# Pairs 6 and 7 moved by DMA as well, and another order of steps, in a chunked attention followed by a multiplicative feed-forward layer

## The chip, the core and the metric

The kernel runs on one core of one Trainium2 chip. The metric is the device time of the whole kernel in microseconds: 244.46 us, the median of 3 runs (244.41 to 244.48).

## What is computed

```python
def _attn_ref(q, k, v):                       # 8 batches, 8 heads, 576 rows, 64 wide
    B, H, S, D = q.shape
    chunk = 64
    nc = S // chunk                            # 9 chunks in each batch
    scale = 1.0 / np.sqrt(D)
    ...
    scores = scale * np.matmul(q_c, k_c.transpose(0, 1, 2, 4, 3))
    scores = scores - np.max(scores, axis=-1, keepdims=True)
    attn = np.exp(scores)
    attn = attn / (np.sum(attn, axis=-1, keepdims=True) + 1e-09)
    out = np.matmul(attn, v_c)
    return out.reshape(B, H, S, D)

def _moe_ref(x, w1, w2, w3, w_out):            # 4608 tokens, 512 -> 1024 -> 1024 -> 512
    a = x @ w1
    b = x @ w2
    h = a * b @ w3
    return h @ w_out

x = attn_out.transpose(0, 2, 1, 3).reshape(B * S, H * D)
```

## The kernel before

The 4608 tokens are cut into 18 *pairs* of 256 tokens (four chunks of 64), and two pairs make a *group* of 512. Pairs 0 to 3 go through the feed-forward layer one by one, later ones a group at a time, under the name of the group's first pair (4, 6, 8, to 16). There is no loop in the usual sense: the string ORDER (lines 9 to 40) lists every step of the kernel, and lines 447 and 448 issue them from left to right. Every instruction is kept in that order on its own engine, so ORDER is five queues woven into one. A step is a letter, a pair (or group) number and, after a point, a part:

- On GpSimd's queue (POOL), loads: `q`, `k`, `v` of a pair (lines 149 and 165, issued at line 98); `i`, `h`, `o` the weights; `x` (line 161) a one-element copy that makes the queue wait until a pair's normalised result is there.
- On VectorE (DVE): `T` transposes q (part 0) or k (part 1) of a pair in 32x32 blocks (line 201); `N` takes the reciprocal of the row sums and multiplies (lines 261 and 264), halves 0 and 1; `X` transposes the result to the layer's input (lines 297 and 305); `M` multiplies the copy of a with b (line 366); `V` transposes w3 (line 407).
- On TensorE (PE), all at line 95: `S` the scores, `P` the weighted sum of v, `A` and `B` the products with w1 and w2 for one eighth of the 1024 columns (of a group; one quarter for a single pair), `W` the product of w3 and w_out into one 1024x512 matrix, `O` the output product of a pair.
- On ScalarE (ACT): `E` the exponential (line 234), `C` the copy of A's result to SBUF (line 351), `Y` the copy of O's result (line 396), `Z` the copy of W's.
- On SyncE (SP), DMAs at line 193: `G` and `H`, below, and `Q`, the store of a pair's output.

The block transposes leave 32 rows of a head on one set of 32 partitions and the other 32 on another. For pairs 0 to 7 the score product runs on such 32-row blocks, two of them added up, 64 products for a pair, and `P` on 32-column blocks, 64 products too. From pair 8 on, `G` (line 205) moves q and k of a group between partitions, part 0 and part 1 with four DMAs of 128 KB each, so that `S` has 32 products of 64 rows, and `P` 32 products of 64 columns; `X` then writes to a tile `xm`, and `H` (line 310) moves it to the layer's input with eight DMAs of 64 KB in two parts. The conditions `p < 8` and `p >= 8` (lines 219, 247, 295, 328 and 360) make the choice.

Buffers set most waits between the engines. PSUM is one pool of four tiles, each of two banks (line 88): one tile serves an `S` until its `E` is done, each half of a `P` until its `N`, an `O` until its `Y`, a `W` until its `Z`, and a column part of the layer from its `A` until its `M`. `A` writes the first half of its tile, `B` the second, `C` reads the first half, `M` the copy and the second half. Copies of a have three buffers (line 350), o_sb two, qkT, qkm and xm two each, xt four, q and k five, v six (line 115; pair p uses buffer p modulo 6).

In the order before, each column part is issued as A, B, C, M.

Of the kernel before, what the change touches and what calls it, by code (L numbers as in the profile page):

```python
# [8 lines left out]
ORDER = """  # L9
R0 R1 v0 q1 k1 i0 v1 i1 i2 q2 k2 v2 i3 q3 k3 v3 q4 k4 v4 o h0 h1 D0.0.0.16.64 K0 T0.0 K1 T0.1 q5 k5  # L10
v5 S0 T1.0 E0 P0 D0.1.0.4.512 T1.1 q6 k6 v6 N0.0 S1 D1.0.0.5.512 X0.0 N0.1 X0.1 A0.0 E1 B0.0 C0.0 P1
M0.0 A0.1 N1.0 X1.0 B0.1 C0.1 N1.1 A0.2 X1.1 B0.2 C0.2 M0.1 A1.0 T2.0 B1.0 C1.0 M0.2 A1.1 T2.1 q7 k7
v7 B1.1 C1.1 M1.0 S2 M1.1 A0.3 E2 T3.0 B0.3 C0.3 P2 M0.3 A1.2 N2.0 X2.0 B1.2 C1.2 N2.1 A1.3 X2.1
B1.3 C1.3 M1.2 A2.0 T3.1 q8 k8 v8 B2.0 C2.0 M1.3 S3 T4.0 A2.1 E3 M2.0 B2.1 T4.1 q9 k9 C2.1 P3 v9
M2.1 A2.2 N3.0 B2.2 C2.2 X3.0 A2.3 N3.1 B2.3 X3.1 C2.3 M2.2 S4 M2.3 A3.0 E4 B3.0 C3.0 A3.1 M3.0 B3.1
C3.1 V0 A3.2 M3.1 B3.2 C3.2 V1 A3.3 M3.2 B3.3 C3.3 V2 W0 M3.3 V3 W1 Z0 V4 V5 W2 Z1 V6 V7 T5.0 Z2 W3
T5.1 q10 k10 T6.0 T6.1 P4 v10 q11 k11 Z3 S5 N4.0 O0 E5 X4.0 N4.1 X4.1 T7.0 O1 T7.1 Y0 Q0 T8.0 P5 v11
q12 k12 Y1 S6 T8.1 O2 Q1 E6 N5.0 X5.0 N5.1 X5.1 O3 T9.0 T9.1 Y2 G4.0 P6 v12 q13 k13 A4.0 N6.0 B4.0
G4.1 Y3 X6.0 N6.1 C4.0 A4.1 X6.1 B4.1 C4.1 M4.0 Q2 S7 Q3 M4.1 A4.2 E7 T10.0 B4.2 C4.2 T10.1 P7 v13
q14 k14 A4.3 M4.2 B4.3 N7.0 C4.3 A4.4 X7.0 M4.3 B4.4 C4.4 N7.1 A4.5 M4.4 B4.5 C4.5 X7.1 S8 M4.5 S9  # L20
E8 A4.6 T11.0 B4.6 E9 T11.1 P8 v14 q15 k15 C4.6 A4.7 M4.6 G5.0 B4.7 C4.7 N8.0 A6.0 M4.7 B6.0 N8.1
C6.0 G5.1 A6.1 X8.0 B6.1 M6.0 C6.1 X8.1 P9 v15 A6.2 M6.1 N9.0 B6.2 C6.2 N9.1 A6.3 M6.2 B6.3 C6.3
X9.0 A6.4 M6.3 B6.4 C6.4 X9.1 A6.5 T12.0 H4.0 B6.5 C6.5 M6.4 A6.6 M6.5 B6.6 T12.1 H4.1 C6.6 S10 S11
M6.6 E10 A6.7 T13.0 B6.7 E11 P10 T13.1 C6.7 O4 M6.7 G6.0 N10.0 N10.1 X10.0 G6.1 P11 Y4 X10.1 O5
N11.0 N11.1 x11 q16 k16 v16 Q4 X11.0 X11.1 T14.0 A8.0 H5.0 Y5 B8.0 T14.1 C8.0 A8.1 M8.0 B8.1 H5.1
C8.1 T15.0 A8.2 B8.2 M8.1 C8.2 T15.1 Q5 A8.3 B8.3 C8.3 M8.2 G7.0 S12 M8.3 S13 E12 A8.4 T16.0 B8.4
E13 G7.1 P12 T16.1 C8.4 A8.5 B8.5 M8.4 C8.5 N12.0 A8.6 M8.5 B8.6 C8.6 N12.1 x12 q17 k17 v17 A8.7
M8.6 B8.7 C8.7 X12.0 P13 M8.7 A10.0 X12.1 B10.0 C10.0 N13.0 A10.1 M10.0 B10.1 N13.1 C10.1 A10.2
X13.0 B10.2 M10.1 C10.2 X13.1 S14 S15 M10.2 E14 A10.3 H6.0 T17.0 B10.3 E15 P14 T17.1 C10.3 A10.4
H6.1 M10.3 B10.4 C10.4 N14.0 A10.5 M10.4 B10.5 G8.0 C10.5 N14.1 A10.6 M10.5 B10.6 C10.6 X14.0 P15  # L30
G8.1 X14.1 A10.7 M10.6 B10.7 N15.0 C10.7 O6 N15.1 M10.7 X15.0 X15.1 H7.0 S16 Y6 S17 O7 E16 E17 H7.1
P16 Y7 O8 Q6 N16.0 Q7 N16.1 X16.0 X16.1 P17 Y8 A12.0 N17.0 Q8 B12.0 N17.1 C12.0 A12.1 X17.0 B12.1
M12.0 C12.1 X17.1 A12.2 M12.1 H8.0 B12.2 C12.2 A12.3 M12.2 B12.3 C12.3 H8.1 A12.4 M12.3 B12.4 C12.4
A12.5 M12.4 B12.5 C12.5 A12.6 M12.5 B12.6 C12.6 A12.7 M12.6 B12.7 C12.7 O9 M12.7 O10 Y9 Q9 A14.0 Y10
B14.0 C14.0 Q10 A14.1 M14.0 B14.1 C14.1 A14.2 M14.1 B14.2 C14.2 A14.3 M14.2 B14.3 C14.3 A14.4 M14.3
B14.4 C14.4 A14.5 M14.4 B14.5 C14.5 A14.6 M14.5 B14.6 C14.6 A14.7 M14.6 B14.7 C14.7 O11 M14.7 O12
Y11 Q11 A16.0 Y12 B16.0 C16.0 Q12 A16.1 M16.0 B16.1 C16.1 A16.2 M16.1 B16.2 C16.2 A16.3 M16.2 B16.3
C16.3 A16.4 M16.3 B16.4 C16.4 A16.5 M16.4 B16.5 C16.5 A16.6 M16.5 B16.6 C16.6 A16.7 M16.6 B16.7
C16.7 O13 M16.7 O14 Y13 Q13 O15 Y14 Q14 O16 Y15 Q15 Y16 Q16 O17
"""  # L40
# [4 lines left out]

@with_exitstack
def first_path(
# [305 lines left out]
    def do_M(p, j):  # L353
        g = p // 2
        if g not in ab_t:
            ab_t[g] = msb.tile([P, FO, GT], bf, tag="ab", bufs=3, name="ab")
# [9 lines left out]
        inorder(nc.vector.tensor_mul(o, view(a_t.pop((p, j))[:]), view(ps_t.pop((p, j))[:, 1, :])))  # L366
# [201 lines left out]
```

## Time and profile before

| | us |
|---|---|
| median of 3 runs | 244.46 |
| span of the profiled execution | 242.9 |
| PE, first to last product | 1.44 to 239.66 |
| DVE busy | 154.3 |
| ACT busy | 85.2 |
| POOL busy | 83.7 |

The profile is of one execution. Its span runs from the first to the last instruction; the time of a run lies a little above it, 1.56 us if the median is set beside this span. The slices of the span, 40 equal ones of 6.07 us each, show busy tenths by engine (9 is 90% or more), the granted TensorE clock and the DMA share:

```
PE   1189989999999999999999999999999999999994
DVE  1756799699799588999998899918540332143000
ACT  2412423423333344425336234162332332322322
POOL 7856976656986345764160230000000000000000
PEclk9999999999999999999999999999999999999999
DMA  6999999999999999999999793735502200400244
```

PE is full from the fourth slice on. DVE is nearly full until slice 25 (about 152 us), where the attention ends, and light behind it. The DMA engines are full until slice 22 (about 133 us), most of it q0, the loads of q, k, v and the weights.

### The profile page before, as it was taken

How to read it: one execution, taken by the hardware profiler on the slowest of the kernel's cores; microseconds unless marked ns; L12 is line 12 of the kernel's file. 1: busy time of each engine (PE TensorE's matmuls, PEld its weight loads, DVE VectorE, ACT ScalarE, POOL GpSimd, SP SyncE). 2: the span in 40 equal slices, each digit the busy share in tenths (PEclk: the TensorE clock that was granted, in tenths of full speed). 3: DMA queues.
4: the chain of work that ended last, by engine and by line, in shares of the span. 5: the costliest groups of instructions: out<-in, count | busy, mean ns of one | idle time of the engine just before them, and what ended most of it. 6: DMA issues, size and time to landing. Idle time of an engine off the chain costs nothing.

```text
span 242.9 us, 6385 instructions
## 1 busy us (share of the span) xinstructions
PE 226.7 (93%) x2753; PEld 120.2 (49%) x2753; DVE 154.3 (64%) x235; ACT 85.2 (35%) x116; POOL 83.7 (34%) x114
## 2 busy tenths in 40 slices
PE   1189989999999999999999999999999999999994
PEld 1147868874445444444444444444444444444443
DVE  1756799699799588999998899918540332143000
ACT  2412423423333344425336234162332332322322
POOL 7856976656986345764160230000000000000000
PEclk9999999999999999999999999999999999999999
DMA  6999999999999999999999793735502200400244
GB/s 173 179 185 181 185 169 200 196 193 171 167 173 218 222 228 259 179 224 196 205 236 223 221 139 91 163 88 209 142 0 89 87 0 0 173 3 1 86 173 173
DMA packets 93597, 37.65 MB, mean 155 GB/s; under 512 B 75008, under 2 KB 86528, under 8 KB 93568
## 3 DMA queue, kind: packets, MB, share of 16 engines
q0 software_dynamic: 82592, 18.88, 83.9%
q1 hardware_dynamic: 9936, 17.83, 24.0%
q10 hardware_dynamic: 1040, 0.52, 0.8%
q8 instruction: 21, 0.34, 0.6%
q14 instruction: 8, 0.07, 0.1%
HBM read 38.80 MB, written 9.44 MB: 199 GB/s over the span
## 4 chain that ended last, share of the span: by engine, by line
PE 72%; DMA 16%; DVE 4%; SPq 3%; POOL 2%; issue 1%; ACT 0%; DVEq 0%; POOLq 0%
PE ab_ps L95 39%; PE o_ps L95 23%; PE w_ps L95 6%; DMA w<-in_moe_w_dram 4%; DMA qkm<-qkT 3%; SPq L193 3%; DMA qk<-in_q_dram 3%; DMA qk<-in_k_dram 3%; DMA xt<-xm 3%; PE pv L95 2%; PE s_ps L95 2%; DVE qkT L201 2%; POOL vbuf L98 1%; POOL w L98 1%; DVE xt L297 1%
## 5 line engine op out<-in xcount | busy, mean ns | idle before, releaser
L95 PE MATMUL ab_ps<-xt,w 128*128 128x512 bf16 (+1 forms) x688 | 127.4, 342 | 0.7 <-DVE xt L297 0.6
L95 PEld LDWEIGHTS <-w 128*128 128x128 bf16 x704 | 67.1, 98 | 56.1 <-issue 1.8
L366 DVE TENSOR_TENSOR ab<-a_sb,ab_ps 128x512 bf16<-128x512 f32 x71 | 47.8, 674 | 43.4 <-ACT a_sb L351 43.1
L351 ACT COPY a_sb<-ab_ps 128x512 f32<-128x512 f32 x71 | 41.6, 586 | 81.3 <-PE ab_ps L95 81.0
L95 PE MATMUL o_ps<-w3o,ab 128*128 128x512 bf16 (+1 forms) x296 | 63.9, 373 | 0.0
L201 DVE STREAM_TRANSPOSE qkT<-qk 128x1024 bf16<-128x1024 bf16 x36 | 45.1, 1291 | 7.2 <-ACT qk L144 5.5
L95 PEld LDWEIGHTS <-ab 128*128 128x128 bf16 x296 | 28.5, 98 | 32.2
L98 POOL DMA_DIRECT2D vbuf<-in_v_dram x40 | 33.9, 855 | 20.4 <-DMA qk<-in_q_dram 5.2
L396 ACT COPY o_sb<-o_ps 128x1024 f32<-128x1024 f32 x17 | 17.2, 1012 | 45.3 <-PE o_ps L95 41.3
L264 DVE TENSOR_TENSOR xn<-pv,rcs 128x512 bf16<-128x512 f32 x36 | 24.9, 692 | 1.4
L98 POOL DMA_DIRECT2D qk<-in_q_dram x23 | 18.1, 790 | 8.9 <-DMA qk<-in_k_dram 2.4
L98 POOL DMA_DIRECT2D qk<-in_k_dram x23 | 18.0, 783 | 6.5 <-DMA vbuf<-in_v_dram 3.7
L234 ACT ACTIVATE e<-s_ps 128x1024 bf16<-128x1024 f32 x16 | 15.9, 1026 | 1.7 <-PE s_ps L95 1.3
L95 PE MATMUL w_ps<-wo,w3T 128*128 128x512 bf16 x64 | 14.0, 379 | 0.0
L305 DVE STREAM_TRANSPOSE xm<-xn 128x512 bf16<-128x512 bf16 x20 | 13.5, 696 | 0.2
L261 DVE RECIPROCAL rcs<-pv 128x8 f32<-128x8 f32 x36 | 6.9, 193 | 10.4 <-PE pv L95 10.4
L98 POOL DMA_DIRECT2D w<-in_moe_w_dram x16 | 11.1, 695 | 5.3 <-DMA wo<-in_moe_w_out_dram 2.9
L95 PEld LDWEIGHTS <-e 64*32 64x32 bf16 (+1 forms) x832 | 7.8, 97 | 8.7 <-issue 6.9
L95 PE MATMUL pv<-vbuf,e 64*32 64x65 bf16 (+1 forms) x832 | 10.2, 197 | 1.8 <-ACT e L234 1.1
L297 DVE STREAM_TRANSPOSE xt<-xn 128x512 bf16<-128x512 bf16 x16 | 11.4, 711 | 0.5
L389 DVE COPY o_sb<-o_ps 128x256 f32<-128x256 f32 x1 | 0.4, 425 | 16.0 <-PE o_ps L95 16.0
L95 PEld LDWEIGHTS <-qkT 32*64 32x64 bf16 x512 | 5.5, 117 | 10.1 <-DVE qkT L201 7.9
(29 smaller groups left out, 54.2 us busy)
## 6 DMA issues: line engine op xcount, KB each, us to landing
out_dram<-o_sb SPq DMA_DIRECT2D x17, 512.0 KB, 3.3
qkm<-qkT SPq DMA_DIRECT2D x40, 128.0 KB, 4.0
vbuf<-in_v_dram POOLq DMA_DIRECT2D x32, 128.0 KB, 8.2
w<-in_moe_w_dram POOLq DMA_DIRECT2D x16, 256.0 KB, 9.9
qk<-in_q_dram POOLq DMA_DIRECT2D x11, 256.0 KB, 6.8
qk<-in_k_dram POOLq DMA_DIRECT2D x11, 256.0 KB, 7.8
xt<-xm SPq DMA_DIRECT2D x40, 64.0 KB, 3.2
wo<-in_moe_w_out_dram POOLq DMA_DIRECT2D x4, 256.0 KB, 7.1
```

Source lines behind the costliest of these rows:

```text
L95: return inorder(nc.tensor.matmul(*a, **kw))
L98: return inorder(nc.gpsimd.dma_start(dst, src))
L193: inorder(nc.sync.dma_start(dst, src))
L201: inorder(nc.vector.transpose(qkT_t[g][:, :, p % 2, s, heads(h)].rearrange("p e h (y t) -> p h t e y", t=2), qk_t[p][:, s, heads(h)].rearr ...
L234: inorder(nc.scalar.activation(e_t[p][:, :, heads(hh)], s_t[p][:].rearrange("p u (h q) -> p u h q", q=CH)[:, :, heads(hh)], Exp, scale=sca ...
L261: inorder(nc.vector.reciprocal(rc, pv[:, :, :, D:W]))
L264: inorder(nc.vector.tensor_mul(xn_t[p][:, u], pv[:, :, :, 0:D], rc.to_broadcast([P, 2, 4, D])))
L297: inorder(nc.vector.transpose(new_xt(g)[:].rearrange("p (o t) -> p o t", o=KO)[:, :, t0:t0 + UT] .rearrange("p o (m y) -> p m o y", y=BL), ...
L305: inorder(nc.vector.transpose(xm_t[g][:, u, :, m].rearrange("p o (c y) -> p c o y", y=BL), xn_t[p][:].rearrange("p u r m d -> p (u r) m d" ...
L351: inorder(nc.scalar.copy(a_t[p, j][:], ps_t[p, j][:, 0, :]))
L366: inorder(nc.vector.tensor_mul(o, view(a_t.pop((p, j))[:]), view(ps_t.pop((p, j))[:, 1, :])))
L396: inorder(nc.scalar.copy(o_sb[:], ps_t.pop(p)[:]))
```

## The change

The constant MOVED, 6, takes the place of 8 in the five conditions, so pairs 6 and 7 (group 3) use the moved form: S and P of 32 products, X into xm, and the steps G3.0, G3.1, H3.0, H3.1. The v buffers are handed out from a list in the order in which P gives them back. The string ORDER is written anew: for each letter the pairs come in the same order as before, but the letters are woven together in another way.

```diff
+MOVED = 6
...
+    vb_t, vb_free = {}, list(vbuf)
+
     def load_v(p):
+        vb_t[p] = vb_free.pop(0)
...
-                load(vbuf[p % 6][at * CH:(at + m) * CH, u, :, 0:D],
+                load(vb_t[p][at * CH:(at + m) * CH, u, :, 0:D],
...
-            if p < 8:
+            if p < MOVED:
...
         e = e_t[p]
+        vb_free.append(vb_t[p])
...
-                               rhs=vbuf[p % 6][half[r], u, 2 * g + m % 2, 0:W], start=True, stop=True)
+                               rhs=vb_t[p][half[r], u, 2 * g + m % 2, 0:W], start=True, stop=True)
...
-        if p >= 8:
+        if p >= MOVED:
```

The order is the same up to B0.2. Its lines behind that, as far as they are needed here (two of the old ones, then new ones):

```diff
-M0.0 A0.1 N1.0 X1.0 B0.1 C0.1 N1.1 A0.2 X1.1 B0.2 C0.2 M0.1 A1.0 T2.0 B1.0 C1.0 M0.2 A1.1 T2.1 q7 k7
-v7 B1.1 C1.1 M1.0 S2 M1.1 A0.3 E2 T3.0 B0.3 C0.3 P2 M0.3 A1.2 N2.0 X2.0 B1.2 C1.2 N2.1 A1.3 X2.1
...
+M0.0 A0.1 N1.0 X1.0 B0.1 C0.1 N1.1 A0.2 X1.1 B0.2 M0.1 C0.2 A1.0 A1.1 B1.0 T2.0 T2.1 q7 B1.1 S2 M0.2
+C1.0 C1.1 A0.3 E2 M1.0 P2 k7 B0.3 M1.1 A1.2 N2.0 C0.3 A1.3 B1.2 N2.1 X2.0 T3.0 C1.2 B1.3 X2.1 T3.1
+C1.3 A2.0 M0.3 C2.0 B2.0 M1.2 q8 S3 A2.1 M1.3 A2.2 M2.0 E3 P3 T4.0 C2.1 C2.2 B2.1 N3.0 B2.2 N3.1
...
+T6.0 E4 T6.1 Z2 P4 T7.0 S5 T7.1 N4.0 Z3 k10 O0 T8.0 O1 q11 E5 N4.1 X4.0 Y0 G3.0 q12 X4.1 Y1 k11 P5
+v8 N5.0 N5.1 O2 Q0 X5.0 X5.1 G3.1 A4.0 O3 T8.1 C4.0 Y2 S6 E6 S7 T9.0 T9.1 Q1 B4.0 T10.0 M4.0 A4.1
+G4.0 T10.1 E7 P6 Y3 B4.1 v9 N6.0 C4.1 N6.1 A4.2 G4.1 C4.2 B4.2 M4.1 X6.0 M4.2 A4.3 P7 q13 q14 N7.0
+Q2 B4.3 C4.3 A4.4 N7.1 k12 B4.4 M4.3 A4.5 X6.1 C4.4 C4.5 B4.5 A4.6 k13 k14 C4.6 M4.4 A4.7 S8 T11.0
+v10 B4.6 B4.7 M4.5 q15 X7.0 X7.1 M4.6 C4.7 S9 M4.7 E8 P8 N8.0 O4 E9 N8.1 Q3 P9 Y4 H3.0 O5 T11.1 X8.0
+T12.0 H3.1 v11 T12.1 Y5 N9.0 T13.0 A6.0 G5.0 B6.0 N9.1 X8.1 C6.0 X9.0 A6.1 C6.1 B6.1 T13.1 A6.2 B6.2
+X9.1 M6.0 G5.1 A6.3 C6.2 H4.0 H4.1 q16 M6.1 B6.3 A6.4 M6.2 B6.4 C6.3 S10 M6.3 v12 C6.4 G6.0 E10 A6.5
+T14.0 T14.1 M6.4 C6.5 B6.5 A6.6 M6.5 C6.6 B6.6 A6.7 C6.7 P10 M6.6 S11 N10.0 B6.7 A8.0 B8.0 E11 Q4
...
+P13 C10.0 v14 M10.0 C10.1 B10.1 N13.0 N13.1 A10.2 M10.1 X12.0 A10.3 B10.2 X12.1 C10.2 C10.3 q17
+A10.4 M10.2 B10.3 x12 G7.0 B10.4 X13.0 G7.1 C10.4 A10.5 v15 k17 M10.3 X13.1 M10.4 x11 A10.6 S14 S15
+T16.1 T17.0 T17.1 B10.5 C10.5 B10.6 C10.6 E14 O6 M10.5 Q5 M10.6 E15 P14 N14.0 N14.1 G8.0 Y6 X14.0 O7
+Y7 P15 G8.1 A10.7 H6.0 B10.7 S16 C10.7 N15.0 E16 N15.1 X14.1 X15.0 v16 v17 S17 M10.7 O8 E17 H6.1 Q6
+Y8 P16 A12.0 B12.0 N16.0 A12.1 C12.0 M12.0 P17 B12.1 C12.1 N16.1 A12.2 C12.2 X15.1 B12.2 N17.0 H7.0
+A12.3 C12.3 Q7 N17.1 M12.1 B12.3 A12.4 B12.4 M12.2 C12.4 A12.5 B12.5 M12.3 C12.5 M12.4 A12.6 Q8
...
+C14.7 M14.6 Q11 M14.7 B16.0 A16.1 A16.2 C16.0 A16.3 B16.1 M16.0 C16.1 M16.1 A16.4 C16.2 C16.3 B16.2
+C16.4 M16.2 A16.5 B16.3 O12 Y12 M16.3 C16.5 B16.4 A16.6 O13 Y13 M16.4 A16.7 B16.5 M16.5 C16.6 C16.7
+Q12 B16.6 O14 B16.7 M16.6 Q13 O15 Y14 Q14 Y15 Q15 M16.7 O16 Y16 Q16 O17
```

In the old order the same stretches read `A4.2 E7 T10.0 B4.2 C4.2`, `S8 M4.5 S9 E8 A4.6 T11.0 B4.6 E9 T11.1 P8` and `T17.0 B10.3 E15 P14 T17.1 C10.3 A10.4 H6.1 M10.3`.

More of the change, by code (lines that the diff above doesn't have):

```diff
@@ L16 @@
[L16 to L37, printed above, removed]
@@ L38 @@
-C16.3 A16.4 M16.3 B16.4 C16.4 A16.5 M16.4 B16.5 C16.5 A16.6 M16.5 B16.6 C16.6 A16.7 M16.6 B16.7
-C16.7 O13 M16.7 O14 Y13 Q13 O15 Y14 Q14 O16 Y15 Q15 Y16 Q16 O17
+M0.0 A0.1 N1.0 X1.0 B0.1 C0.1 N1.1 A0.2 X1.1 B0.2 M0.1 C0.2 A1.0 A1.1 B1.0 T2.0 T2.1 q7 B1.1 S2 M0.2
+C1.0 C1.1 A0.3 E2 M1.0 P2 k7 B0.3 M1.1 A1.2 N2.0 C0.3 A1.3 B1.2 N2.1 X2.0 T3.0 C1.2 B1.3 X2.1 T3.1
+C1.3 A2.0 M0.3 C2.0 B2.0 M1.2 q8 S3 A2.1 M1.3 A2.2 M2.0 E3 P3 T4.0 C2.1 C2.2 B2.1 N3.0 B2.2 N3.1
+A2.3 B2.3 X3.0 X3.1 A3.0 M2.1 C2.3 M2.2 k8 A3.1 M2.3 B3.0 B3.1 T4.1 C3.0 q9 M3.0 C3.1 M3.1 A3.2 v7
@@ new lines @@
+T12.0 H3.1 v11 T12.1 Y5 N9.0 T13.0 A6.0 G5.0 B6.0 N9.1 X8.1 C6.0 X9.0 A6.1 C6.1 B6.1 T13.1 A6.2 B6.2
+X9.1 M6.0 G5.1 A6.3 C6.2 H4.0 H4.1 q16 M6.1 B6.3 A6.4 M6.2 B6.4 C6.3 S10 M6.3 v12 C6.4 G6.0 E10 A6.5
+T14.0 T14.1 M6.4 C6.5 B6.5 A6.6 M6.5 C6.6 B6.6 A6.7 C6.7 P10 M6.6 S11 N10.0 B6.7 A8.0 B8.0 E11 Q4
+G6.1 N10.1 C8.0 M6.7 M8.0 X10.0 X10.1 k15 P11 A8.1 A8.2 B8.1 N11.0 B8.2 k16 A8.3 C8.1 C8.2 N11.1
+X11.0 B8.3 A8.4 M8.1 v13 B8.4 S12 C8.3 M8.2 S13 C8.4 H5.0 X11.1 M8.3 A8.5 E12 A8.6 C8.5 M8.4 B8.5
@@ new lines @@
+C8.6 T15.0 H5.1 B8.6 A8.7 B8.7 T15.1 M8.5 E13 P12 M8.6 A10.0 T16.0 B10.0 N12.0 C8.7 A10.1 N12.1 M8.7
+P13 C10.0 v14 M10.0 C10.1 B10.1 N13.0 N13.1 A10.2 M10.1 X12.0 A10.3 B10.2 X12.1 C10.2 C10.3 q17
+A10.4 M10.2 B10.3 x12 G7.0 B10.4 X13.0 G7.1 C10.4 A10.5 v15 k17 M10.3 X13.1 M10.4 x11 A10.6 S14 S15
+T16.1 T17.0 T17.1 B10.5 C10.5 B10.6 C10.6 E14 O6 M10.5 Q5 M10.6 E15 P14 N14.0 N14.1 G8.0 Y6 X14.0 O7
+Y7 P15 G8.1 A10.7 H6.0 B10.7 S16 C10.7 N15.0 E16 N15.1 X14.1 X15.0 v16 v17 S17 M10.7 O8 E17 H6.1 Q6
@@ new lines @@
+Y8 P16 A12.0 B12.0 N16.0 A12.1 C12.0 M12.0 P17 B12.1 C12.1 N16.1 A12.2 C12.2 X15.1 B12.2 N17.0 H7.0
+A12.3 C12.3 Q7 N17.1 M12.1 B12.3 A12.4 B12.4 M12.2 C12.4 A12.5 B12.5 M12.3 C12.5 M12.4 A12.6 Q8
+C12.6 A12.7 H7.1 B12.6 B12.7 O9 C12.7 Y9 M12.5 M12.6 A14.0 B14.0 C14.0 M12.7 M14.0 A14.1 C14.1 A14.2
+B14.1 A14.3 X16.0 C14.2 Q9 B14.2 X16.1 O10 Y10 M14.1 X17.0 H8.0 B14.3 A14.4 Q10 C14.3 X17.1 A14.5
+M14.2 B14.4 C14.4 O11 Y11 A14.6 C14.5 M14.3 M14.4 A14.7 H8.1 A16.0 C14.6 B14.5 B14.6 B14.7 M14.5
+C14.7 M14.6 Q11 M14.7 B16.0 A16.1 A16.2 C16.0 A16.3 B16.1 M16.0 C16.1 M16.1 A16.4 C16.2 C16.3 B16.2
@@ L246, in do_P @@
             for m in range(4):
-                if p < 8:
+                if p < MOVED:
                     for g in range(NB) if hh is None else (2 * hh, 2 * hh + 1):
@@ L255, in do_P @@
                         mm(pv[half[g], r, m * W:(m + 1) * W], lhsT=e[half[r], u, 4 * g + m, :],
-                           rhs=vbuf[p % 6][half[r], u, 4 * g + m, 0:W], start=True, stop=True)
+                           rhs=vb_t[p][half[r], u, 4 * g + m, 0:W], start=True, stop=True)
     def do_N(p, u):
@@ L294, in do_X @@
         g, m = divmod(p, 2)
-        if p < 8:
+        if p < MOVED:
             t0 = m * PT + u * UT
@@ L359, in do_M @@
             view = lambda t: t.rearrange("p (j t) -> p j t", j=2)
-        elif p < 8:
+        elif p < MOVED:
             o = ab_t[g][:, j]
```

3 lines of the change are left out of this document (1 added, 2 removed).

## The prediction

> **What bounds the kernel now.** I read the page's busy rows first, then the chain of waits, then the timelines of PE, ACT, DVE and SP. The busy rows and the chain's shares (page, parts 1 and 4):
>
> ```profile
> PE 226.7 (93%) x2753; PEld 120.2 (49%) x2753; DVE 154.3 (64%) x235; ACT 85.2 (35%) x116; POOL 83.7 (34%) x114
> ...
> PE 72%; DMA 16%; DVE 4%; SPq 3%; POOL 2%; issue 1%; ACT 0%; DVEq 0%; POOLq 0%
> ```
>
> PE is busy for all but 16 us of 242.9. The PE timeline puts 11.3 us of that ahead of 24.3 us and 3.2 us behind the last product (239.66); between, PE stands still for about 1.6 us. So from 24.3 us on, whatever PE does not do is a gain, and whatever holds PE is a loss of the same size. The step prices come from the chain (start, us, what) and the PE timeline:
>
> ```profile
> 187.82 13.81 PE ab_ps L95 x64
> ...
> 74.14 0.72 PE L95 MATMUL pv<-vbuf,e 64*32 64x65 bf16 x64
> 74.79 0.71 PE L95 MATMUL s_ps<-qkT 32*64 32x64 bf16 x64
> ...
> 130.50 0.71 PE L95 MATMUL s_ps<-qkm 64*64 64x64 bf16 x64
> ...
> 132.97 0.45 PE L95 MATMUL pv<-vbuf,e 64*64 64x65 bf16 x32
> ```
>
> One A or B of four 512-column products is 13.81/16 = 0.863 us on PE; one of eight 256-column products (pairs 0 to 3) is 0.89 (64 of them take 7.09 at 45.03). One product lasts 379 ns (the group's mean) and the next starts 216 ns after it, so the last one drains 0.16 us after PE could go on.
>
> What happens behind a product, from one instruction-by-instruction timeline (start, us, engine, line, operation):
>
> ```profile
> 123.50 4.70 PE L95 MATMUL ab_ps<-xt,w 128*128 128x512 bf16 x21
> ...
> 125.42 0.59 ACT L351 COPY a_sb<-ab_ps 128x512 f32<-128x512 f32 x1 [0.71 <-PE ab_ps L95]
> 126.04 0.69 DVE L366 TENSOR_TENSOR ab<-a_sb,ab_ps 128x512 bf16<-128x512 f32 x1 [0.27 <-ACT a_sb L351]
> ```
>
> A8.0 starts at 123.50, so its last product could be followed at 124.36, B8.0's at 125.23. The copy C8.0 reads only A's half of the tile, yet starts at 125.42, after B. So with the order A, B, C the copy waits for B; M ends 1.5 us after B's last issue (0.2 + 0.59 + 0.02 + 0.69). PE meanwhile works on other tiles.
>
> A wait PE to ACT to PE, and a queue held in order:
>
> ```profile
> 10.94 1.03 ACT L234 ACTIVATE e<-z_ps 128x1024 bf16<-128x1024 f32 x1 [2.74 <-PE z_ps L95]
> ...
> 12.02 0.75 PE L95 MATMUL pv<-vbuf,e 64*32 64x65 bf16 x64 [1.13 <-ACT e L234]
> ...
> 30.64 1.31 DVE L201 STREAM_TRANSPOSE qkT<-qk 128x1024 bf16<-128x1024 bf16 x1 [1.32 <-DMA qk<-in_q_dram]
> 31.86 0.65 DVE L366 TENSOR_TENSOR ab<-a_sb,ab_ps 128x512 bf16<-128x512 f32 x1
> ...
> 30.40 0.46 PE L95 MATMUL pv<-vbuf,e 64*32 64x65 bf16 x37
> 31.53 0.30 PE L95 MATMUL pv<-vbuf,e 64*32 64x65 bf16 x27 [0.67 <-issue]
> ```
>
> PE stood 1.13 us for a 1.03 us activation: both hand-overs cost 0.10 together. M0.3 (31.86) stood behind T3.0, which waited for its load, though its copy ended at 31.10: the engines keep their order. The last two rows are P2, held until 31.53 by the last part of v2.
>
> **The change part by part.** All is summed along PE, against the span.
>
> *Less work.* S6 and S7 go from 64 products (0.645 us between neighbours) to 32 (0.32, two pairs are x64 in 0.64); P6 and P7 from 0.63 to 0.38. Together -1.15 us. PE is full there (80 to 90 us), so this is kept.
>
> *C between A and B.* The new order often has A C B. As C waited for B by tile, not by half, so B's first product now waits for C: the built program has this wait at 27 of the B steps and at none before. Price of a bare site (B next after A on PE): drain 0.16 + copy 0.59 + hand-overs 0.10 = 0.85 us. Between 0.59 (copy alone) and 0.95 (with a weight load of 98 ns); I take 0.85, since the wait is on the product, its weights loaded. Bare are B2.0, B4.2, B4.5, B6.1, B6.6, B12.2, B12.3: 7 x 0.85 = +5.95. At B6.5 ACT first does C6.4 (0.59) and E10 (1.03), then C6.5: B6.4's end + 0.2 + 0.59 + 1.03 + 0.6 + 0.05 = 2.5, against S10 and A6.5 (1.2): +1.25. Partly covered: B10.1 (P13's 0.38 of 0.85) +0.4; B10.3 and B16.2, where ACT does C10.2 or C16.1 first, which wait for the B before: 1.46 against one A of 0.86, +0.6 each; B6.7 and B16.6 +0.1 each. Sum +1.8. The other 14 have at least one whole A or other work of 0.86 in between and cost nothing.
>
> Row and rule: the row 125.42 shows a copy that waits for a product in the other half. The Trainium skill (PSUM — Partial Sum Buffer, "PSUM bank collisions raise a hardware error") asks only for guards by bank and quadrant, and the halves are two banks; by it no B need wait, and these 9.0 us would be nothing.
>
> *ACT's order.* C4.7 now stands ahead of E8. C4.7 waits for B4.7, E8 only for the earlier S8. P8 needs E8: 0.2 + 0.59 + 1.03 + 0.05 = 1.87 after B4.7; PE has S9 (0.32): +1.55.
>
> *DVE's order.* T16.1, T17.0, T17.1 now stand between M10.4 and M10.5, and O6 takes the PSUM buffer that M10.5 frees. M10.4 ends 1.5 after B10.4, three transposes at 1.2 (four in 4.80 at 69.53), M10.5 0.6: 5.7. PE has A10.5, A10.6, S14, S15, B10.5, B10.6: 4.1. +1.65. P17 takes the buffer that M12.0 frees, 1.5 after B12.0, with only A12.1 (0.86) between: +0.65. Likewise A8.2 behind M8.0 +0.2, and P6 behind E6 and E7 +0.1.
>
> *P2 ahead of B0.3.* v2's loads and all before are unchanged, so P2's second half still begins at 31.53, but B0.3 (0.89) no longer lies in front: +0.98; the 0.29 us that A2.0 waited for X2.1 goes, T3.0 having moved behind X2.0: net +0.7.
>
> *SP.* G3 and H3 are new: 8 moves each, 128 and 64 KB. At 0.63 to 0.9 us an issue and 3 to 4 us to land they need 9 to 11 us from the last transpose. Along PE's new order G3 (from T7.1, about 69) has 15 us to S6, G4 (82) 16 to S8, H3 (98) 12 to A6.0, H4 16, G5 13. H5 has 7 from X11.1 to A10.0, with 6.5 needed (four issues, the other four gone out after X11.0, and 3.2); H6 stands behind G8, which waits for T17.1, and has about 0.5 to spare at A12.0. Q0 to Q8 are past or between them and hold 0.5 each. I take 0. The bounds are these:
>
> ```profile
> xt<-xm SPq DMA_DIRECT2D x40, 64.0 KB, 3.2
> ...
> 126.97 6.53 DMA xt<-xm
> ```
>
> With 6.53 instead of 3.2, up to +6 at A10.0, S16 and A12.0.
>
> *POOL.* Loads are issued in a new order with the same buffers. q7 to k9 go ahead of v8, so T7.0 may wait about 1 us for q7 on DVE; N4.0 behind it is 1.8 ahead of O1, so PE sees nothing. q13 waits for T8.1 (80), 30 us ahead of T13.0. x12 now gates v15, k17: k17 goes out 3.3 us after N12.1 and lands within 7.8 (median); T17.1 comes 12.5 after. If later, O6 waits as much longer.
>
> *Sum.* -1.15 + 5.95 + 1.25 + 1.8 + 1.55 + 1.65 + 0.95 + 0.7 = +12.7. Span 242.9 + 12.7 = 255.6. The runs' median is 1.56 above the profiled span (244.46), the profiled run's own time is not on the page; I add the same: **257.2 us**.
>
> **Rivals.** (1) *The copies cost nothing* (0.08): B does not stand for C, as two banks would allow. The 9.0 us of the second part go: 248.2. For it: the halves never overlap. Against: 125.42, and the built waits.
>
> (2) *Late moves* (0.11): the 6.53 of a move among loads at A10.0, S16 and A12.0: 263. Against: x12 holds the loads back, so the queue is empty there.
>
> (3) *The queues do not hold* (0.04): ACT and DVE take what is ready, so C4.7 does not hold E8, T17.1 not M10.5, and the copies are through before PE asks. Then only the work counts: -1.15, and the 0.67 and 0.29 of idle: 242.4, faster. It decides if all new stands together are under 2.1 us. Against: M0.3 behind T3.0.
>
> (4) *The clock falls* (0.03): after the 7.36 us that PE stood at the start, nine 512-column products took 489 ns on average instead of 379, 1 us in all. If each of some 13 stands did so: 270. Against: they are under 1.7 us, and the granted clock reads 9 in all 40 slices. The Trainium skill (TensorE: Matmul & The Clock Gate, "A second HAM failure mode: psum-queue depth-cycling") tells of short gaps between groups that make the clock swing; no row here shows it.
>
> **How the numbers follow.** Forecast 0.74 (own range 254 to 260.5: eight sites at 0.59 and O6 1 us less, or half of the late moves). Left out below are rivals 1 and 3 (0.12), above rival 4 and the far half of 2, so 251.5 to 262.5. Same means within 0.2% (0.5 us), about what a measurement can tell: 0.02, between rival 3 and the rest; faster 0.04; slower 0.94.
>
> **What would show it.** In the new profile PE idle before ab_ps products with releaser ACT a_sb L356, 0.7 us each and 0.85 from pitch, at the sites named; one idle of 1.5 before a pv (ACT e) near 101 us and one before o_ps (DVE ab) near 160; a chain with ACT a_sb in it several times, where now it is 0%. PE busy should fall by about 1. It is wrong if PE runs on through B4.2, or if the gaps stand instead behind SP's moves.

## The result, and the profile after

| | before | after |
|---|---|---|
| median of the runs, us | 244.44 (244.24 to 244.48) | 254.46 (254.1 to 255.28) |
| ratio to before, 95% interval | | 1.0416 [1.0396, 1.0437] |
| profiled execution: its own time, us | not shown (median of the first three 244.46) | 255.28 |
| its span, us | 242.9 | 253.7 |
| last product ends, us | 239.66 | 250.44 |

The kernel became 4.2% slower. The median grew by 10.0 us; the span of the profiled execution, the longest of the four, by 10.8, and all of it lies before the end of the last product. The busy rows and the chain's shares of the kernel after (page, parts 1 and 4):

```profile
PE 228.2 (90%) x2625; PEld 119.2 (47%) x2625; DVE 154.0 (61%) x235; ACT 83.7 (33%) x116; POOL 83.7 (33%) x114
...
PE 78%; DVE 8%; ACT 6%; DMA 4%; issue 2%; DVEq 0%; SPq 0%
...
L96 PE MATMUL ab_ps<-xt,w 128*128 128x512 bf16 (+1 forms) x688 | 129.7, 342 | 7.8 <-ACT a_sb L356 6.3
```

No engine got more to do: DVE, ACT and POOL are as busy as before, and PE has 128 products less. PE's busy time did not fall, since the page counts the drain of the last product before each stand as busy (some 0.16 us each time). ACT, which had 0% of the chain, has 6%. The last line is the group of all w1 and w2 products: PE stood 7.8 us ahead of them, 6.3 of it for `a_sb`, the copy of A's result, which no step but M reads.

Where PE stands, from its timeline (start, us, what, products; in brackets the idle time before and what ended it):

```profile
31.36 0.27 PE L96 MATMUL pv<-vbuf,e 64*32 64x65 bf16 x19 [1.09 <-issue]
...
102.23 0.45 PE L96 MATMUL pv<-vbuf,e 64*64 64x65 bf16 x32 [1.23 <-ACT e L238]
...
110.87 2.75 PE L96 MATMUL ab_ps<-xt,w 128*128 128x512 bf16 x12 [0.69 <-DMA qkm<-qkT]
...
122.57 1.89 PE L96 MATMUL ab_ps<-xt,w 128*128 128x512 bf16 x8 [0.73 <-ACT a_sb L356]
...
152.68 3.62 PE L96 MATMUL ab_ps<-xt,w 128*128 128x512 bf16 x16 [0.30 <-ACT a_sb L356]
...
160.09 3.61 PE L96 MATMUL o_ps<-w3o,ab 128*128 128x512 bf16 x16 [1.32 <-DVE ab L371]
```

In order these are P2, P8, A6.0, B6.5, B10.3 and O6. Not in the list are B2.0, B4.2, B4.5, B6.1, B6.6, B12.2 and B12.3 (0.67 each, for `a_sb`), and B10.1 and B16.2, which look like B10.3 (0.30 each); P17's second half has 0.28, A12.0 0.21, and P2 another 0.17 ahead of its first product. One site close up, B4.2, with all engines (start, us, engine, what):

```profile
87.69 0.81 PE L96 MATMUL ab_ps<-xt,w 128*128 128x512 bf16 x3
...
88.54 0.58 ACT L356 COPY a_sb<-ab_ps 128x512 f32<-128x512 f32 x1 [0.28 <-PE ab_ps L96]
...
89.17 1.02 PE L96 MATMUL ab_ps<-xt,w 128*128 128x512 bf16 x4 [0.67 <-ACT a_sb L356]
```

A4.2's last product ends at 88.50, the copy C4.2 runs from 88.54 to 89.12, and B4.2 starts at 89.17. B writes the other half of the tile than the copy reads, and still it waits for the whole copy. The wait is written into the program: the trace has, at the first product of B4.2, a wait for a semaphore of ACT, raised at 89.13 as the copy ended.

The stands of the two timelines account for the loss. Each counts with 0.16 us of drain, as the prediction counted it: the 18 stands behind 25 us in after sum to 11.3 + 18 x 0.16 = 14.2, the three in before (P2 0.67, A2.0 0.29, S7 0.49) to 1.45 + 3 x 0.16 = 1.9. With 1.15 us less work the difference is 14.2 - 1.9 - 1.15 = 11.1, against 10.8 measured.

### The profile page after: what moved, and what is told of

The parts are those of the page before. It is cut to its first block, busy times and chain, and to the rows that moved or that the text cites. A ratio compares the mean times of both kernels' runs of the same rounds, so it can differ in the third digit from the quotient of the medians.

```text
span 253.7 us, 6185 instructions
## 1 busy us (share of the span) xinstructions
PE 228.2 (90%) x2625; PEld 119.2 (47%) x2625; DVE 154.0 (61%) x235; ACT 83.7 (33%) x116; POOL 83.7 (33%) x114
## 4 chain that ended last, share of the span: by engine, by line
PE 78%; DVE 8%; ACT 6%; DMA 4%; issue 2%; DVEq 0%; SPq 0%
PE ab_ps L96 43%; PE o_ps L96 22%; PE w_ps L96 5%; ACT a_sb L356 4%; DVE qkT L205 4%; PE z_ps L96 3%; PE pv L96 3%; DMA raw<-in_q_dram 2%; DMA qkm<-qkT 2%; PE s_ps L96 2%; DVE ab L371 2%; ACT e L238 2%; DVE xn L269 1%; DVE xt L302 1%; ACT qk L145 0%
## 5 line engine op out<-in xcount | busy, mean ns | idle before, releaser
L96 PE MATMUL ab_ps<-xt,w 128*128 128x512 bf16 (+1 forms) x688 | 129.7, 342 | 7.8 <-ACT a_sb L356 6.3
L356 ACT COPY a_sb<-ab_ps 128x512 f32<-128x512 f32 x71 | 41.0, 587 | 88.7 <-PE ab_ps L96 85.3
L96 PE MATMUL o_ps<-w3o,ab 128*128 128x512 bf16 (+1 forms) x296 | 64.7, 374 | 1.3 <-DVE ab L371 1.3
L310 DVE STREAM_TRANSPOSE xm<-xn 128x512 bf16<-128x512 bf16 x24 | 16.0, 691 | 0.1
L99 POOL DMA_DIRECT2D w<-in_moe_w_dram x16 | 11.1, 694 | 5.2 <-DMA vbuf<-in_v_dram 2.0
L96 PEld LDWEIGHTS <-w3T 128*128 128x128 bf16 x64 | 6.3, 98 | 7.3
L412 DVE STREAM_TRANSPOSE w3T<-w 128x1024 bf16<-128x1024 bf16 x8 | 9.5, 1225 | 0.1
```

What stands on the lines that cost most here:

```text
L96: return inorder(nc.tensor.matmul(*a, **kw))
L99: return inorder(nc.gpsimd.dma_start(dst, src))
L310: inorder(nc.vector.transpose(xm_t[g][:, u, :, m].rearrange("p o (c y) -> p c o y", y=BL), xn_t[p][:].rearrange("p u r m d -> p (u r) m d" ...
L356: inorder(nc.scalar.copy(a_t[p, j][:], ps_t[p, j][:, 0, :]))
L412: inorder(nc.vector.transpose(w3T_t[f][:].rearrange("p k (f y) -> p f k y", y=BL), w3[:, NB * f:NB * (f + 1), :].rearrange("p f (k x) -> p ...
```

## The experiments

Each was timed against the kernel before on its own chip, so the ratio is what compares them. The orders are given by the steps that move.

**1. All copies behind their B.** In the new order the 28 C steps that stand between their A and B go right behind B; nothing else changes.

```diff
-N6.1 A4.2 G4.1 C4.2 B4.2 M4.1
+N6.1 A4.2 G4.1 B4.2 C4.2 M4.1
...
-A12.3 C12.3 Q7 N17.1 M12.1 B12.3
+A12.3 Q7 N17.1 M12.1 B12.3 C12.3
```

> The changed kernel (254.46) with each of the 28 copies C that stood between A and B moved to just behind its B; nothing else differs. Theory (a product B stands for the copy of its own tile): the eight stands of 0.67 to 0.73 before ab_ps and the three of 0.30 go, each with 0.16 us of drain, 6.0 + 0.9 + 1.8 = 8.7, less up to 1 us where M now frees its PSUM tile 0.6 us later: 246 to 247. Rival (the stands only uncover another limit, the moves between partitions or DVE): a part of it comes back at A6.0, A10.0 or A12.0, 249 or more. Rival (copies cost nothing, it is the weaving): within 1 us of 254.5.

Measured: 248.25 us, ratio 1.0144 [1.0121, 1.0166]: 6.6 us less than after by the ratios (0.0272 x 244.4), 7.2 by the spans of the profiled executions (246.5). PE's stands behind 25 us are now these, and two short ones, 0.16 ahead of P2 and 0.15 ahead of S11:

```profile
31.37 0.27 PE L96 MATMUL pv<-vbuf,e 64*32 64x65 bf16 x19 [1.08 <-issue]
85.93 0.52 PE L96 MATMUL pv<-vbuf,e 64*64 64x65 bf16 x32 [0.47 <-DVE ab L371]
100.35 0.45 PE L96 MATMUL pv<-vbuf,e 64*64 64x65 bf16 x32 [1.23 <-ACT e L238]
108.62 8.79 PE L96 MATMUL ab_ps<-xt,w 128*128 128x512 bf16 x40 [0.32 <-DMA xt<-xm]
154.99 3.61 PE L96 MATMUL o_ps<-w3o,ab 128*128 128x512 bf16 x16 [1.65 <-DVE ab L371]
172.81 0.32 PE L96 MATMUL pv<-vbuf,e 64*64 64x65 bf16 x16 [0.28 <-DVE ab L371]
```

No stand for `a_sb` is left. The eleven of after came to 6.3 + 11 x 0.16 = 8.1 us, and 7.2 of span came back: C4.0, now behind B4.0, makes M4.0 later and costs P6 0.47, and O6 stands 0.33 longer. The time lies between the 246 to 247 expected and the first rival's 249. About two thirds of the loss is the place of the copies; the rest, some 3.6 us of span, is elsewhere in the new order.

**2 and 3. The same edit in the kernel before.** Only there C goes ahead of B: in group 14 (8 sites), then in groups 12, 14 and 16 (24 sites), where nothing but A, B, C, M and O runs.

```diff
-A14.1 M14.0 B14.1 C14.1 A14.2 M14.1 B14.2 C14.2
+A14.1 M14.0 C14.1 B14.1 A14.2 M14.1 C14.2 B14.2
```

> The kernel before (244.44) with the copies C14.0 to C14.7 put between their A and B: eight bare sites, PE's and DVE's orders untouched. Theory: 8 x 0.84 = +6.7, 251.1, with eight stands of 0.67 us before ab_ps, released by the copy. Rival (the tile's halves are two banks, so B does not stand): 244.4.

> As the last, with the 24 copies of groups 12, 14 and 16: 24 x 0.84 = +20.2, 264.6, three times the effect of eight. Rival (many short stands make the TensorE clock fall): more than that, and a granted clock below 1; rival (no wait): 244.4.

Measured: 251.22 us, ratio 1.0268 [1.0244, 1.0292] with 8 sites, and 265.32, 1.0831 [1.0809, 1.0853] with 24. From the ratios that is 0.0268 x 244.96 / 8 = 0.82 us a site, and 0.0831 x 244.96 / 24 = 0.85: the prediction's price for a bare site, and it adds up site by site. The waits of the 24-site kernel (who waited for what: us in all, times, longest):

```profile
PE ab_ps L95 <- ACT a_sb L351: 17.1, 24, 1.5
```

One stand for each edited site, in a kernel that had none. The granted clock stayed at 1.0 with a stand every 2.56 us. The Trainium skill (PSUM — Partial Sum Buffer, "PSUM bank collisions raise a hardware error") asks for guards by bank and quadrant only; here the two halves of a tile are two banks, and the built program guards them as one. The measurement decides: a copy between A and B costs 0.83 us of PE's time, whatever the banks would allow.

**4. The three transposes behind M10.6.** In the new order T16.1, T17.0 and T17.1 no longer stand ahead of M10.5, on which O6 waits.

```diff
-S15 T16.1 T17.0 T17.1 B10.5 C10.5 B10.6 C10.6 E14 O6 M10.5 Q5 M10.6 E15
+S15 B10.5 C10.5 B10.6 C10.6 E14 O6 M10.5 Q5 M10.6 T16.1 T17.0 T17.1 E15
```

> The changed kernel (254.46) with T16.1, T17.0 and T17.1 moved from ahead of M10.5 to behind M10.6; nothing else. Theory (O6 stands for M10.5, which stands behind the three transposes): the stand of 1.3 us before o_ps, 1.5 with the drain, goes, and G8, 1.2 us later, still lands ahead of S16: 253.0. Rival (S16 or A12.0 then stands for the moves, as H6 follows G8 on SP): 254 to 256, with a stand before S16 or A12.0.

Measured: 257.7 us, ratio 1.0526 [1.0498, 1.0554]: slower than after by 1%, and above the rival's 254 to 256, with the stands that the rival named. PE's timeline there:

```profile
159.25 3.61 PE L96 MATMUL o_ps<-w3o,ab 128*128 128x512 bf16 x16 [0.53 <-DVE ab L371]
...
170.49 0.93 PE L96 MATMUL s_ps<-qkm 64*64 64x64 bf16 x63 [1.33 <-DMA qkm<-qkT]
...
176.26 2.75 PE L96 MATMUL ab_ps<-xt,w 128*128 128x512 bf16 x12 [0.91 <-DMA xt<-xm]
...
180.25 0.32 PE L96 MATMUL pv<-vbuf,e 64*64 64x65 bf16 x16 [0.89 <-DVE ab L371]
```

O6's stand fell from 1.32 to 0.53, so the three transposes did hold it. But T17.1 ended near 163.6 instead of 159.5, and SP's queue behind it slid along: G8 went out at 163.70 (159.55 in after), H6 at 168.70 (164.57). S16 then stood 1.33 for G8 and A12.0 0.91 for H6, and the store Q6 behind H6 held Y8, C12.0 and M12.0, for which P17 stood 0.89. That the prediction gave H6 only half a microsecond to spare is borne out: four microseconds of delay at its head cost three on PE.

**5. P2 behind B0.3, as in the old order.**

```diff
-A0.3 E2 M1.0 P2 k7 B0.3 M1.1
+A0.3 E2 M1.0 k7 B0.3 P2 M1.1
```

> The changed kernel (254.46) with P2 moved back behind B0.3, nothing else. Theory: B0.3 again lies in front of the wait for v2, so P2's idle falls by 0.9 and all behind comes 0.9 earlier: 253.5. Rival (the 0.9 is taken up by the next wait, V0 for the weights' load or X2.1): 254.2 or more.

Measured: 254.89 us, ratio 1.0428 [1.04, 1.0456]: no gain. P2 and B2.0 in PE's timeline:

```profile
31.65 0.30 PE L96 MATMUL pv<-vbuf,e 64*32 64x65 bf16 x27 [0.53 <-issue]
37.90 1.03 PE L96 MATMUL ab_ps<-xt,w 128*128 128x256 bf16 x8 [1.37 <-ACT a_sb L356]
```

P2's break is shorter (0.53 for 1.09), and B2.0 stands 0.70 longer. The trace shows the next wait: the copy C2.0 stood 1.09 us for DVE, since M0.3, which gives a copy buffer back, is behind N2, X2 and T3 there, and that chain reached it 0.35 us later than in after. What moved is where in P2 the break falls: 19 products are left behind it in after, 27 here, as in before. The eight products of B0.3 that changed sides are the difference, so the break keeps its place in PE's stream of products, not in P2.

**6. E8 ahead of C4.7.**

```diff
-M4.6 C4.7 S9 M4.7 E8 P8
+M4.6 E8 C4.7 S9 M4.7 P8
```

> The changed kernel (254.46) with E8 moved ahead of C4.7 on ACT, nothing else. The prediction's term says that P8 stands for E8 behind C4.7; undone it should give back 1.2 to 1.4: 253.1. Rival: P8 also waits for the PSUM tile that M4.7 frees, which ends 1.5 us after B4.7, against 1.67 measured for P8's start; then only 0.1 to 0.2 is gained, 254.3, and the stand before P8 is named for DVE instead of ACT.

Measured: 254.49 us, ratio 1.0401 [1.0371, 1.043], the same as after. PE's timeline:

```profile
102.28 3.61 PE L96 MATMUL o_ps<-w3o,ab 128*128 128x512 bf16 x16 [0.75 <-DVE ab L371]
...
110.59 2.75 PE L96 MATMUL ab_ps<-xt,w 128*128 128x512 bf16 x12 [0.76 <-DMA xt<-xm]
```

P8's stand of 1.23 is gone, but O4 right behind P8 now stands 0.75 for M4.7, a wait that P8's stand had hidden, and A6.0 still stands 0.76 for H3's moves (0.69 in after). The wait that the prediction priced at 1.55 was the first of two that end at nearly the same time. The rival's time (254.3) came, with M4.7 as the cause, though the stand is ahead of O4 and not of P8.

**7. The new order without the moved form.** Pairs 6 and 7 again as in before, G3 and H3 left out.

```diff
-MOVED = 6
+MOVED = 8
...
-X4.0 Y0 G3.0 q12 X4.1 Y1 k11 P5
+X4.0 Y0 q12 X4.1 Y1 k11 P5
```

> The changed kernel's order with MOVED = 8 and the steps G3.0, G3.1, H3.0, H3.1 taken out, so pairs 6 and 7 run in the old form; all else as in the new order. Theory: S6, S7, P6, P7 cost 1.15 more on PE again, but the stand of 0.69 us (0.85 with the drain) before A6.0, which waits for H3, goes: +0.3, 254.8. Rival (the move is worth its 1.15 in full): 255.6. Rival (G3 and H3 hold up the other moves on SP): the time falls, below 254.

Measured: 261.48 us, ratio 1.0705 [1.0669, 1.0741]. A6.0's stand is gone with H3, but the comparison is spoiled by one line of PE's timeline, inside P6:

```profile
90.51 0.23 PE L96 MATMUL pv<-vbuf,e 64*32 64x65 bf16 x9 [4.00 <-issue]
```

In the middle of a run of 64 products PE stood 4.00 us for nothing that this timeline shows. All six runs of this kernel took over 259.8 us, so it isn't a chance of one run. The profiled execution (259.87 us, span 258.3) is 4.6 us above after's span, and its timeline accounts for that: 4.16 for this break with its drain, 1.3 for a fall of the granted clock behind it (B4.1 to P7 took 5.67 us, in after 4.39), and 1.15 for the work that comes back; against these, A6.0's stand (0.85), P2's longer break (0.83) and A12.0's stand (0.37) are gone. So the two terms of the expectation, 1.15 and 0.85, are both there, but the break hides them, and how long it was in the other five executions isn't known. By these two terms the moved form is worth about 0.3 us in the new order; the time of this run can't show so little.

**8. The breaks.** The break of P2 and that of P6 have the releaser "issue". Counting the products ahead of every break of this kind over all traces gives the same few numbers, in whatever place they fall:

```
products ahead of the break   before     after      1        4        5          6          7          9
223                           A0.0 1.12  A0.0 0.44                    A0.0 0.18  A0.0 0.62  A0.0 0.45  A0.0 0.17
478                           P2 0.67    P2 1.09    P2 1.08  P2 1.08  P2 0.53    P2 1.08    P2 0.26    P2 0.92
606                                                                                                    S3 0.45
1372                          S7 0.49                                                       P6 4.00
```

(The columns are the kernels, by experiment; 9 is the mended order below; idle time in us. 2 and 3 break at 223, 478 and 1372 as before does, 10 and 11 at 478. The break in A0.0 ends by 18.8 us and costs nothing in before and after: A1.0, which waits for X1.1, starts at 24.3 us in both, and also in experiment 1, which has no such break.) A12.0's 0.21 in after and 0.24 in experiment 6 read "issue" as well, but the trace shows another cause: PE's queue works there through the waits for H6's eight moves, in steps of 0.1 us from 174.21 on, the last move having landed at 174.16.

To test it, the kernel before got eight more zero products early in its warm-up, which move every later product up by eight numbers.

```diff
-D1.0.0.5.512
+D1.0.0.13.512
```

> The kernel before with 13 zero products instead of 5 ahead of A0.0, so that each later product of PE has a number higher by 8. Theory (the breaks with the releaser issue lie at fixed numbers of PE's products, 478 and 1372 in every trace so far, whatever work stands there): P2 breaks after 29 of its 64 products instead of 37, S7 after 43 instead of 51, each by 0.2 to 1.1 us. Rival (P2 stands for the last part of v2, S7 for its operand): the breaks stay after 37 and 51. Time: eight 512-column products take 8 x 0.216 = 1.7 us, less what PE idled ahead of A0.0's second half: 244.4 to 246.2 by both.

Measured: 245.26 us, ratio 1.0034 [1.0018, 1.005]. S7 in PE's timeline:

```profile
87.41 0.54 PE L95 MATMUL s_ps<-qkT 32*64 32x64 bf16 x43
88.48 0.37 PE L95 MATMUL s_ps<-qkT 32*64 32x64 bf16 x21 [0.54 <-issue]
```

S7 now breaks behind its 43rd product instead of its 51st, eight earlier, as the theory said. P2's break did not show in this trace (its 64 products ran on in 0.70 us), so that half of the expectation is neither met nor contradicted. A break of this kind stays at its number, and its length varies from nothing to 4 us; the last section says what it ends with.

**9. A mended order.** The new order with all copies but C4.0 behind their B, P2 behind B0.3, T16.1 behind M10.2, T17.1 behind M10.5, P17 behind B12.1, and the steps around P8 so that A4.7 hides E8:

```diff
-C4.6 M4.4 A4.7 S8 T11.0 v10 B4.6 B4.7 M4.5 q15 X7.0 X7.1 M4.6 C4.7 S9 M4.7 E8 P8
+M4.4 B4.6 C4.6 S8 T11.0 v10 A4.7 E8 B4.7 M4.5 q15 X7.0 X7.1 M4.6 C4.7 S9 P8 M4.7
```

> The changed kernel with all named stands mended: A B C at every site but C4.0, P2 behind B0.3, T16.1 ahead (behind M10.2) and T17.1 behind M10.5, P17 behind B12.1, and around P8 the order A4.6 B4.6 S8 A4.7 B4.7 S9 P8 O4, so that O4 stands only for M4.7. If the terms are right and add up: the old order (244.44), less 1.15 of work, less 0.29 and 0.49 of idle that the new order does not have, plus 0.8 (O4 behind M4.7) and 0.3 (A6.0 behind H3): 243.6. Rival (the weaving itself costs in small waits that only show when the large ones are gone): 245 or more.

Measured: 245.96 us, ratio 1.0059 [1.0034, 1.0083]: not the 243.6 of the terms, but the rival's 245 or more. But it was not many small waits that made the difference. Besides the breaks at products 478 and 606 and 0.15 ahead of S11, these remained:

```profile
99.84 3.61 PE L96 MATMUL o_ps<-w3o,ab 128*128 128x512 bf16 x16 [0.75 <-DVE ab L371]
108.48 8.79 PE L96 MATMUL ab_ps<-xt,w 128*128 128x512 bf16 x40 [1.10 <-ACT o_sb L401]
...
151.48 0.45 PE L96 MATMUL s_ps<-qkm 64*64 64x64 bf16 x32 [0.26 <-DVE ab L371]
154.29 3.61 PE L96 MATMUL o_ps<-w3o,ab 128*128 128x512 bf16 x16 [0.53 <-DVE ab L371]
```

These are O4, A6.0, S15 and O6. A6.0's releaser reads ACT's copy of an O. But H3's last move was issued by 101.97 and the moves took 5.3 to 7.1 us to land, so the moves are the other candidate. The trace speaks for the moves: A6.0 takes O4's tile, whose copy Y4 ended at 104.51 (the copy that ended just before A6.0 is Y5), while H3's last move landed at 108.14. Experiment 11 tests it.

**10. The moved form alone.** The order before, with G3 and H3 put in and only the room made that they need.

```diff
-T6.0 T6.1 P4 v10 q11 k11 Z3 S5 N4.0 O0 E5 X4.0 N4.1 X4.1 T7.0 O1 T7.1 Y0 Q0
+T6.0 T6.1 T7.0 T7.1 G3.0 G3.1 P4 v10 q11 k11 Z3 S5 N4.0 O0 E5 X4.0 N4.1 X4.1 O1 Y0 Q0
...
-T10.1 P7 v13 q14 k14 A4.3 M4.2 B4.3 N7.0 C4.3 A4.4 X7.0 M4.3 B4.4 C4.4 N7.1 A4.5 M4.4 B4.5 C4.5 X7.1
+P7 v13 q14 k14 N7.0 M4.2 N7.1 X7.0 H3.0 X7.1 H3.1 A4.3 B4.3 C4.3 A4.4 M4.3 T10.1 B4.4 C4.4 A4.5 M4.4 B4.5 C4.5
```

> The moved form alone: before's order and its A, B, C sequence, with S, P, X of pairs 6 and 7 in the moved form and the steps G3 and H3 put in; to make room, T7 goes ahead of N4, S6 and E6 behind O3, P7 a little ahead, P8 behind B4.7, all else between pair 5 and A6.0 keeps its order. Theory (the form saves PE 1.15 us and every loss of the new kernel lies in its order): span 242.9 - 1.15 = 241.8 and a time near 243.3 if A6.0 finds H3's moves landed; X7.1 should end near 92, eight issues take 5.4, so the last goes out near 97.5 and lands 2 to 7 us later, 99.5 to 104.5, while PE asks for A6.0 near 100: a stand there of 0 to 4.5, a time of 243.3 to 247.8, 245 in the middle. Rival (the moved form itself is dear: its 16 moves slow the loads, and DVE or S6 stands for them): over 248, with PE idle ahead of S6 or behind a transpose that waits for a load.

Measured: 251.22 us, ratio 1.0278 [1.0262, 1.0295]: above the theory's range and in the rival's, over 248. But the place was the one that the theory named, A6.0. The PE timeline, and the granted clock by stretch (last figures of a line: clock, DMA share, GB/s):

```profile
105.98 5.72 PE L96 MATMUL ab_ps<-xt,w 128*128 128x512 bf16 x16 [5.43 <-DVE xm L310]
```

```profile
96.50:100.10 3.60, 3.55 (x30) 1.49 (x17) 1.71 (x2) 2.43 (x3) 1.91 (x3) 1.00 1.30 308
105.90:111.60 5.70, 5.62 (x16) 2.03 (x16) 1.37 (x3) 0.58 (x1) 2.62 (x4) 0.62 1.53 243
112.00:117.00 5.00, 5.00 (x35) 2.29 (x25) 4.23 (x9) 1.49 (x3) 3.06 (x5) 1.00 1.96 171
```

H3's eight moves took from 93.48 to 100.74 to issue and 5.4 to 7.1 to land, so the last was there at 105.63, until when PE's queue stood at the wait for it, and A6.0 started at 105.98; X8.0, which the profile names, only happened to end then: A6.0 reads nothing of it. (Less than half of the stand, up to 102.9, is also covered by a second wait: M4.6, whose tile A6.0 takes, stood behind T11.1, and that 2.88 us for k11. The rival's mechanism, a late load, is there too.) And the stand of 5.43 brought a cost that nobody had put down: the clock fell, to 0.62 in the mean of that stretch, and the 16 products behind it took 5.72 us instead of 3.63, 2.1 us more. So the moved form, worth 1.15 us of PE's work, makes the old order 6.6 us slower, because A6.0 comes too soon behind X7.1. In the new order O4 and O5 stand between them and hide all but 0.69.

**11. The mended order with earlier moves.** To tell apart the two candidates of 9: X7.0, X7.1 and H3 earlier; S14 and S15 behind B10.5.

```diff
-A4.4 N7.1 k12 B4.4 M4.3 A4.5 X6.1 C4.4 B4.5 C4.5 A4.6 k13 k14 M4.4
+A4.4 N7.1 k12 B4.4 X7.0 X6.1 M4.3 H3.0 A4.5 C4.4 B4.5 C4.5 X7.1 A4.6 H3.1 k13 k14 M4.4
...
-A10.6 S14 S15 T17.0 B10.5 C10.5 B10.6
+A10.6 T17.0 B10.5 C10.5 S14 S15 B10.6
```

> The mended version of the run before (245.96 us) with three more edits: X7.0 and X7.1 stand right behind N7.1 on DVE and H3.0, H3.1 go out about 2.5 us earlier, still behind Q2; S14 and S15 stand behind B10.5. Theory (A6.0's stand of 1.10 us there, put down to ACT's copy of O, is the landing of H3's moves, sent from 96.54 to 101.97 and some 6.5 us on the way; O6's 0.53 and S15's 0.26 are M10.5 and M10.4): with H3's last issue near 99.5 the moves land near 106, ahead of A6.0 at 107.4, so 1.10 + 0.53 + 0.26 = 1.9 us go: 244.1, within 0.4 us of before. Rival (A6.0 waits for Y4 by its PSUM tile, as the releaser says): the 1.10 stays and 245.2 results. A second rival: M4.3 and M4.4 are up to 1.3 us later behind X7 and PE stands for them at S8 or A4.7.

Measured: 244.63 us against 244.72 for before on the same chip, ratio 1.0003 [0.9989, 1.0018]. H3 went out from 91.74 to 96.74, 4.8 us earlier, and A6.0, S15 and O6 no longer stand. So A6.0's 1.10 in 9 was the landing of the moves, not the copy that the releaser named. What this order still stands for is in PE's timeline:

```profile
98.67 3.61 PE L96 MATMUL o_ps<-w3o,ab 128*128 128x512 bf16 x15 [0.75 <-DVE ab L371]
120.26 0.45 PE L96 MATMUL s_ps<-qkm 64*64 64x64 bf16 x32 [0.16 <-DVE ab L371]
122.24 1.89 PE L96 MATMUL ab_ps<-xt,w 128*128 128x512 bf16 x8 [0.57 <-DMA qkm<-qkT]
170.22 10.52 PE L96 MATMUL ab_ps<-xt,w 128*128 128x512 bf16 x48 [0.26 <-DVE xn L269]
```

These are O4, S11, A8.0 and A12.2. With drain the four are 1.74 + 4 x 0.16 = 2.4 us; the break at P2 adds 0.29 + 0.16 = 0.45. (The timeline shows 0.16 more, with the releaser "issue", ahead of B4.0; but only seven of the eight products of B4.0 and A4.1 are recorded there, and S6 to P6 takes 2.54 us, in experiment 9 2.53, so a record is missing and PE did not stand.) Before has 1.9 of its own, so 2.4 + 0.45 - 1.9 = 0.95 is lost and 1.15 saved, and the two spans, 242.8 and 242.9, are level. No version here beats the kernel before.

## Why the prediction was right, and where its sizes were off

The direction and the mechanism were right: 257.2 was forecast, 254.46 came, slower by waits of PE that the order makes. The terms against their measured sizes in the profiled executions (each stand with its 0.16 of drain):

| term | forecast, us | measured, us |
|---|---|---|
| less work in S6, S7, P6, P7 | -1.15 | -1.15 (S6 and S7 two pairs in 0.64, P6 and P7 0.38 each) |
| 7 bare sites | +5.95 | 7 x 0.83 = +5.8 |
| B6.5 | +1.25 | +0.9 |
| B10.1, B10.3, B16.2; B6.7, B16.6 | +1.8 | 3 x 0.46 = +1.4; none seen |
| P8 behind E8 behind C4.7 | +1.55 | +1.4 |
| O6 behind the three transposes | +1.65 | +1.5 |
| P17; A8.2 and P6 | +0.65; +0.3 | +0.45; none seen |
| P2, and A2.0's old wait | +0.7 | +0.3 |
| A6.0 behind H3 | 0 | +0.85 |
| A12.0 behind the waits for H6 | 0 | +0.35 |
| the break in S7 of before, absent in after | 0 | -0.65 |
| sum | +12.7 | +11.1 (span: +10.8; medians: +10.0) |

That the sum came so near is in part luck: terms that were too large by 2.1 us together stand against A6.0's 0.85 and A12.0's 0.35, which were put at nothing.

*C between A and B* is shown by three runs: taken away it gives 6.6 us back (7.2 by the spans), put into the kernel before it costs 0.82 and 0.85 a site. The rival in which B does not stand for C falls with them. The single site that was mis-sized most is B6.5, where ACT does C6.4, E10 and C6.5 in a row: I took the durations 0.59 and 1.03, but in after they start at 120.53, 121.01 and 121.93, 0.48 and 0.92 apart. Durations of neighbours overlap; where an engine works without a break, the distance between starts is the price. B10.3 and B16.2 (0.6 forecast, 0.46 found), where ACT also does two copies in a row, were over-sized in the same way.

*ACT's order* and *DVE's order* put the stands where they came, at P8 and at O6. But each was priced as if taking it away gave its price back, and experiments 4 and 6 show that it does not: behind P8's stand lies M4.7's, and the transposes that hold O6 also feed SP's queue. P17 was taken whole, but M12.0 gates only its second half.

*P2* is the step whose cause was wrong. The prediction read "issue" as the landing of v2's last part. Experiment 5 and the zero products show that the break is tied to the number of the product: 478 in every trace that has it. Its releaser, "issue", said that nothing in the profile explained it, P2 broke after 37 products, where no half of v2 begins, and in the trace of before the loads that P2 waits for had landed by 26.49 us, 5 us ahead of the end of the break. The sum was hardly hurt (0.7 against 0.3) only because the break did stay.

*SP* was taken at 0, with late moves as a rival at A10.0, S16 and A12.0. A10.0 and S16 did not stand, and A12.0 only 0.21. The late one was H3 at A6.0, to which the prediction gave 12 us, at 3 to 4 us to land. In after H3's eight issues took 5.43 us from 98.14, and a move took 5.6 to 7.5 us to land, with loads under way: the last landed at 110.52, and A6.0 started at 110.87, behind three more waits in PE's queue of 0.1 us each. (The releaser's name in that row, `qkm<-qkT`, is that of another move; A6.0 does not read it.) The high bound, 6.53, was the right price here, while POOL still loaded.

*The queues do not hold* and *the clock falls* did not happen here: ACT and DVE kept their order, and the page shows the clock at 9 in all 40 slices with 18 stands of up to 1.32 us. Experiments 7 and 10 show that the clock does fall at longer stands.
